# Seven of eight products in the last pass of a fused attention and two feed-forward layers

## The chip, the core and the metric

The kernel runs on one core of one Trainium2 chip. The metric is the device time of one execution in microseconds (us). The engines named here are PE (TensorE matmul), PEld (its weight load), DVE (VectorE), ACT (ScalarE), POOL (GpSimd) and SP (SyncE, which issues the DMAs). Inputs and output are float32.

## What is computed

A banded attention over 1536 tokens (2 batches of 768, 8 heads of 64) gives x of 1536 x 512. Two feed-forward layers of 512 to 2048 to 512 follow. In the reference, cut to what matters:

```python
x = attn_out.transpose(0, 2, 1, 3).reshape(B * S, H * D)      # 1536 x 512
h = np.maximum(x @ w_in, 0.0)                                 # first layer
x = h * h @ w_out
h = x @ w_in                                                  # second layer, beta = 1
g = np.where(h >= beta, h, np.where(h <= -beta, 0.0, (h + beta) ** 2 / (4.0 * beta)))
return g @ w_out
```

## The kernel before

**Three matmuls for one.** A float32 value is held as two fp32r parts, a high part and the rest (`Plan.copy` at L118 makes the high part, on ACT; `Plan.rest` at L130 subtracts it, on DVE). Each product is three matmuls into one sum in PSUM: high by high, low by high, high by low (`MOVING`).

**Chunks.** The 2048 inner columns are cut into 16 chunks of 128. The weights of a chunk (128 rows of `w_in` and of `w_out`, four blocks of 128 each) stand as high and low parts in one of nine slots (`slot0` to `slot8`, `h` and `l`). The program's names carry a further number that only counts tiles (`slot5l_128` is the low part of slot 5). From the second layer on slot 8 is cut up and used for the small g tiles, so eight slots are left.

**Events.** The work is a list of events (`Ffn.__init__`), each one chunk for one range of tokens. An event has a first product `h` (four blocks of 128 by three matmuls, L479), a function on ACT and DVE, and a second product `y` (L532), which adds to banks of PSUM that are kept over all 16 chunks. In the second layer the tokens are done in two passes of 768: tokens 768 to 1535 with the chunks from 15 down to 0, then tokens 0 to 767 with the chunks from 0 up to 15, the last pass. In a pass every chunk has two events: one for 512 tokens (its `h` in bank 0, its `y` in banks 2 to 5) and one for 256 tokens (its `h` in bank 1, its `y` in banks 6 and 7). The last two chunks are put in another order.

**The function of the second layer** (L499, L501, L503) is `max(h, min(r, 1) * r)` with `r = relu(h / 2 + 1 / 2)`: one instruction on ACT, then two on DVE. Two more make the parts of g (L118 on ACT, L130 on DVE). For the 256 tokens r lies in the tile `nat` and g in `slot8`; for the 512 tokens they are `r` and `g`.

**Weights in the last pass.** Chunks 0 to 7 are in the eight slots when the pass begins. Chunks 8 to 15 are read back from DRAM (`kept`, written when they were first made, at L416 to L442) and split again into parts, two halves of 512 each (`Ffn.parts`).

**What sets the order.** The kernel records each operation with a length, a due time and the keys of what it reads and writes. `Plan.emit` then lays out all engines by these lengths and due times and writes the instructions in the order of their planned starts, each engine in order. Which instruction waits for which is settled from that written order: an instruction that touches a tile waits for the ones written before it that touch the same tile in a way that matters. A PSUM bank is one tile.

Of the kernel before, what the change touches and what calls it, by code (L numbers as in the profile page):

```python
# [307 lines left out]
class Ffn:  # L308
# [12 lines left out]

    KF = 16
    CB = 4

    def __init__(self, nc, plan, banks, x, w, half, kept, out):
# [24 lines left out]
        for t0, order in ((768, down), (0, up)):  # L350
            parts = [(n, o) for n in range(self.KF) for o in (0, 512)]

            if not t0:
                parts[-4:] = [(n, o) for o in (512, 0) for n in (self.KF - 2, self.KF - 1)]
            for n, o in parts:
                hb = 1 if o or not t0 and n == self.KF - 1 else 0
                event(1, order[n], t0 + o, 256 if o else 512, hb, [6, 7] if o else y,
                      n == 0, n == self.KF - 1, 256 if o else 512)

        at = 0  # L360
        for e in self.events:
            e["due"] = at
            e["len"] = e["n"] / 512
            at += e["len"]
# [13 lines left out]
    def plan_slots(self, span):  # L378


        holds = [None] * len(self.slots)
        used = [-9] * len(self.slots)
        span = [(first - 9 * (first == 0), end) for first, end in span]
        self.makes = []
        keys = [(e["layer"], e["c"]) for e in self.events]
        for u, key in enumerate(keys):
            slots = [i for i, (first, end) in enumerate(span) if first <= u < end]
            found = [i for i in slots if holds[i] == key]
            if found:
                i = found[0]  # L390
            else:
                later = keys[u:]
                free = [i for i in slots if used[i] < u - 2]
                i = max(free, key=lambda i: (
                    later.index(holds[i]) if holds[i] in later else len(keys), -used[i], -i))
                self.makes.append((u, max(used[i], span[i][0] - 2)))
                holds[i] = key
            self.events[u]["slot"] = i
            used[i] = u


        self.due_makes = [keys[u] for u, _ in self.makes]

    def make_after(self, u):

        while self.makes and self.makes[0][1] <= u:
            self.make(self.makes.pop(0)[0])

    def make(self, u):

        nc, op = self.nc, self.plan.op
        e = self.events[u]
        layer, c, due = e["layer"], e["c"], e["due"]
        kc, f32 = self.ring("whole")
        if (layer, c) in self.stored:
            op("dma", 1456, due - W_LOAD, lambda: nc.sync.dma_start(out=f32, in_=self.kept[c]),  # L416
               [("kept", c)], [(*kc, 0), (*kc, 1)], lag=LAG)
            self.due_makes.pop(0)
            self.parts(u, kc, f32)
            return  # L420
# [22 lines left out]
        later = any(key == (layer, c) for key in self.due_makes[1:])  # L443
# [5 lines left out]
        self.parts(u, kc, f32)  # L449

    def parts(self, u, kc, f32):
        plan = self.plan
        e = self.events[u]
        i = e["slot"]
        sl = self.slots[i]
        for n in range(2):
            src, hi, lo = f32[:, 512 * n:512 * n + 512], sl[0][:, n], sl[1][:, n]
            d = e["due"] - W_MAKE + 0.4 * n
# [7 lines left out]
    def h(self, u):  # L466

        nc, op = self.nc, self.plan.op
        assert all(v != u for v, _ in self.makes)
        e = self.events[u]  # L470
        layer, t0, N, kb, i = e["layer"], e["t0"], e["n"], e["hb"], e["slot"]
# [25 lines left out]
        else:  # L497

            op("act", ns_act(N) + 64, due, lambda: nc.scalar.activation(  # L499
                out=r, in_=hp, func=ACTF.Relu, bias=self.half, scale=0.5), [bank], [kr])  # L500
            op("dve", ns_dve(N), due, lambda: nc.vector.scalar_tensor_tensor(  # L501
                out=r, in0=r, scalar=1.0, in1=r, op0=ALU.min, op1=ALU.mult), (), [kr], port=True)
            op("dve", ns_dve(N), due, lambda: nc.vector.tensor_tensor(  # L503
                out=r, in0=hp, in1=r, op=ALU.max), [bank], [kr])
        self.plan.copy(N, due, g[:, 0], r, [kr], [(*kg, 0)], engines=GCOPY)
        self.plan.rest(N, due, g[:, 1], r, g[:, 0], [kr, (*kg, 0)], [(*kg, 1)], engines=GREST)
        self.g[u] = kg, g

    def y(self, u):

        op, plan, nc = self.plan.op, self.plan, self.nc
        e = self.events[u]
        layer, t0, N, yb, i = e["layer"], e["t0"], e["n"], e["yb"], e["slot"]
# [4 lines left out]
        for t in range(self.CB if layer == 0 else N // P):  # L518
# [40 lines left out]
            else:  # L559
                ko, ot = self.ring("o")  # L560
                r0 = t0 + t * P
                for n in range(2):
                    h = slice(256 * n, 256 * n + 256)
                    way = ("act", "dve")[n]
                    plan.copy(256, due, ot[:, h], o[:, h], [bank], [(*ko, n)], psum=True, engines=(way,))
                op("dma", 728, due, lambda ot=ot, r0=r0: nc.sync.dma_start(
                    out=self.out[r0:r0 + P, :], in_=ot), [(*ko, n) for n in range(2)], (), lag=LAG)

    def run(self, events):

        for u in events:
            if u == 0:
                self.make_after(-1)
                self.h(0)
            if u + 1 < len(self.events):
                self.h(u + 1)
            self.y(u)
            self.make_after(u)

# [380 lines left out]
def kernel(  # L960
# [31 lines left out]
    def tiles(s, f, plan):  # L992
# [24 lines left out]
        f.tiles["o"] = [nat[:, 512 + i * 512:1024 + i * 512] for i in range(7)]  # L1017
        f.later = {
# [13 lines left out]
        }  # L1032
        if plan is None:
            return a
# [129 lines left out]
```

## Time and profile before

| | us |
|---|---|
| median of three runs | 639.33 |
| lowest and highest | 638.82 and 640.70 |
| the profiled execution | 640.03 |
| span in its profile | 638.2 |
| busy in it: PE, DVE, ACT | 625.1, 411.5, 308.3 |

The page of the profile gives busy times and shares; the chain of waits lists what ended last, in order of time; the stretches give busy time between two moments; the timeline lists single instructions with their start and length. Times in the trace count from the span's start. Matmuls overlap in the records, each being shown longer than the distance to the next one, so the pace of PE is read from start to start. The same holds of DVE and ACT where an instruction doesn't depend on the one before it.

### The profile page before, as it was taken

How to read it: one execution, taken by the hardware profiler on the slowest of the kernel's cores; microseconds unless marked ns; L12 is line 12 of the kernel's file. 1: busy time of each engine (PE TensorE's matmuls, PEld its weight loads, DVE VectorE, ACT ScalarE, POOL GpSimd, SP SyncE). 2: the span in 40 equal slices, each digit the busy share in tenths (PEclk: the TensorE clock that was granted, in tenths of full speed). 3: DMA queues.
4: the chain of work that ended last, by engine and by line, in shares of the span. 5: the costliest groups of instructions: out<-in, count | busy, mean ns of one | idle time of the engine just before them, and what ended most of it. 6: DMA issues, size and time to landing. Idle time of an engine off the chain costs nothing.

```text
span 638.2 us, 9469 instructions
## 1 busy us (share of the span) xinstructions
PE 625.1 (98%) x3535; PEld 512.6 (80%) x3535; DVE 411.5 (64%) x949; ACT 308.3 (48%) x668; POOL 30.1 (5%) x57
## 2 busy tenths in 40 slices
PE   7999999999999999999999999999999999999995
PEld 5788987878888888888888888888888888888883
DVE  5899999965459992242299999964443555543443
ACT  3898777855456642232256565533222443332232
POOL 3122020110000000000000000000000000000000
PEclk9999999999999999999999999999999999999998
DMA  7444454430123583000016624121000311100002
GB/s 266 155 156 153 133 150 148 145 139 17 34 99 101 181 251 129 0 1 0 1 33 207 221 67 163 35 67 34 0 1 1 106 61 66 34 1 0 2 1 105
DMA packets 18775, 55.23 MB, mean 87 GB/s; under 512 B 2336, under 2 KB 2336, under 8 KB 18720
## 3 DMA queue, kind: packets, MB, share of 16 engines
q1 hardware_dynamic: 18432, 54.53, 26.0%
q8 instruction: 30, 0.49, 0.3%
q14 instruction: 25, 0.20, 0.1%
q10 hardware_dynamic: 288, 0.00, 0.0%
HBM read 47.19 MB, written 7.34 MB: 85 GB/s over the span
## 4 chain that ended last, share of the span: by engine, by line
PE 94%; DVE 3%; DMA 1%; ACT 1%; issue 0%; ACTq 0%; DVEq 0%
PE bank L479 42%; PE bank L532 41%; PE bank L639 4%; PE bank L726 3%; PE bank L690 3%; DMA words<-in_n_global_dram 1%; DVE pr L662 0%; PE bank L1068 0%; DVE whole L435 0%; DVE whole L439 0%; PE bank L1066 0%; ACT g L118 0%; DVE m L144 0%; DVE whole L432 0%; DVE slot0l L130 0%
## 5 line engine op out<-in xcount | busy, mean ns | idle before, releaser
L501 DVE SCALAR_TENSOR_TENSOR r<-r 128x512 f32<-128x512 f32 x32 | 22.2, 692 | 88.8 <-ACT r L499 88.6
L118 ACT ACTIVATE g<-r 128x512 fp32r<-128x512 f32 (+1 forms) x84 | 51.4, 612 | 50.6 <-DVE r L503 29.1
L495 DVE SCALAR_TENSOR_TENSOR r<-bank,r 128x512 f32<-128x512 f32 (+1 forms) x52 | 33.8, 649 | 61.7 <-ACT r L494 59.7
L130 DVE TENSOR_TENSOR g<-r,g 128x512 fp32r<-128x512 f32 (+1 forms) x84 | 56.0, 667 | 24.2 <-ACT g L118 20.4
L499 ACT ACTIVATE r<-bank,half 128x512 f32<-128x512 f32 x32 | 22.0, 689 | 96.4 <-PE bank L479 96.4
L494 ACT ACTIVATE r<-bank 128x512 f32<-128x512 f32 (+1 forms) x52 | 29.3, 564 | 76.9 <-PE bank L479 75.6
L667 ACT ACTIVATE pr<-pr,mn 128x256 f32<-128x256 f32 (+1 forms) x96 | 45.8, 480 | 11.2 <-DVE mn L662 10.8
L142 ACT ACTIVATE whole<-raw 128x512 f32<-128x512 f32 x50 | 33.4, 675 | 13.6 <-DMA kept<-whole 2.2
L662 DVE CUSTOM_DVE_ANT_0 pr<-bank,m 128x256 f32<-128x256 f32 (+1 forms) x96 | 33.2, 394 | 5.1 <-PE bank L726 5.1
L479 PE MATMUL bank<-x,slot1h 128*128 128x512 f32 (+1 forms) x120 | 34.2, 351 | 0.0
L479 PE MATMUL bank<-x,slot0h 128*128 128x512 f32 (+1 forms) x120 | 34.0, 352 | 0.2 <-DVE x L130 0.2
L439 DVE SCALAR_TENSOR_TENSOR whole<-raw,whole 128x512 uint32<-128x512 uint32 x50 | 34.1, 684 | 0.1
L479 PE MATMUL bank<-x,slot3h 128*128 128x512 f32 (+1 forms) x120 | 34.1, 353 | 0.0
L435 DVE SCALAR_TENSOR_TENSOR whole<-raw,whole 128x512 uint32<-128x512 uint32 x50 | 33.9, 684 | 0.2
L479 PE MATMUL bank<-x,slot2h 128*128 128x512 f32 (+1 forms) x120 | 34.0, 352 | 0.0
L479 PE MATMUL bank<-x,slot4h 128*128 128x512 f32 (+1 forms) x112 | 33.5, 365 | 0.0
L479 PE MATMUL bank<-x,slot6h 128*128 128x512 f32 (+1 forms) x112 | 33.4, 365 | 0.0
L479 PE MATMUL bank<-x,slot5h 128*128 128x512 f32 (+1 forms) x112 | 33.3, 365 | 0.0
L639 PEld LDWEIGHTS bank<-nat 64*128 64x128 f32 x352 | 25.1, 206 | 8.8 <-issue 3.0
L639 PE MATMUL bank<-nat 64*128 64x128 f32 x352 | 29.8, 306 | 2.0 <-DMA nat<-in_q_dram 1.0
L146 POOL TENSOR_SCALAR pr<-pr,mn 128x256 f32<-128x256 f32 (+1 forms) x39 | 25.4, 660 | 130.1 <-DVE mn L674 55.6
L479 PE MATMUL bank<-x,slot7h 128*128 128x512 f32 (+1 forms) x88 | 25.5, 357 | 0.0
(264 smaller groups left out, 1564.4 us busy)
## 6 DMA issues: line engine op xcount, KB each, us to landing
raw<-in_moe_w_in_dram SPq DMA_DIRECT2D x25, 512.0 KB, 3.5
raw<-in_moe_w_out_dram SPq DMA_DIRECT2D x25, 512.0 KB, 4.5
pr<-in_moe_w_in_dram SPq DMA_DIRECT2D x7, 512.0 KB, 3.4
pr<-in_moe_w_out_dram SPq DMA_DIRECT2D x7, 512.0 KB, 4.0
nat<-in_k_dram SPq DMA_DIRECT2D x12, 256.0 KB, 3.8
nat<-in_q_dram SPq DMA_DIRECT2D x12, 256.0 KB, 3.2
nat<-in_v_dram SPq DMA_DIRECT2D x12, 256.0 KB, 3.4
out_dram<-nat SPq DMA_DIRECT2D x12, 256.0 KB, 2.5
```

The source lines that it names most:

```text
L118: ("act", ns_act(n) - 30 * psum, lambda: nc.scalar.activation(out=out, in_=in_, func=ACTF.Copy), False),
L130: ways = [("dve", ns_dve(n), lambda: nc.vector.tensor_tensor(out=out, in0=in_, in1=hi, op=ALU.subtract), not psum)]
L142: ("act", ns_act(n) + (0 if isinstance(by, float) else 107), lambda: nc.scalar.activation(out=out, in_=in_, func=ACTF.Copy, scale=by), False),
L435: op("dve", ns_dve(512), d + 0.2, lambda h=h: nc.vector.scalar_tensor_tensor(out=word[:, h], in0=low[:, h], scalar=29, in1=word[:, h], op0 ...
L439: op("dve", ns_dve(512), d + 0.3, lambda h=h: nc.vector.scalar_tensor_tensor(out=word[:, h], in0=high[:, h], scalar=0x80000000, in1=word[: ...
L479: op("pe", ns_mm(N), due + 0.01 * m, lambda k=k, a=a, b=b, m=m: nc.tensor.matmul(out=hp, lhsT=sl[a][:, 0, k * P:(k + 1) * P], rhs=self.x[: ...
L494: op("act", ns_act(N), due, lambda: nc.scalar.activation(out=r, in_=hp, func=ACTF.Relu), [bank], [kr])
L495: op("dve", ns_dve(N), due, lambda: nc.vector.scalar_tensor_tensor(out=r, in0=hp, scalar=0.0, in1=r, op0=ALU.max, op1=ALU.mult), [bank], [kr])
L532: lambda o=o, lhsT=lhsT, rhs=rhs, n=n: nc.tensor.matmul(out=o, lhsT=lhsT, rhs=rhs, start=(e["first"] and n == 0), stop=(e["last"] and n == 2),
L639: nc.tensor.matmul(**c)
L662: op("dve", ns_dve(w), due, lambda e=e: nc.vector.tensor_tensor_reduce(out=pr[:, e, :w], in0=self.banks[kbs[e % 2]][:, e // 2 * 256:e // 2 ...
L667: op("act", ns_act(w) + 200, due, lambda e=e: nc.scalar.activation(out=pr[:, e, :w], in_=pr[:, e, :w], func=ACTF.Exp, bias=mn[:, e:e + 1], ...
```

## The change

It concerns the last pass alone. Chunks 0 and 1 keep their events. Chunks 2 to 15 go in seven pairs. For a pair the first product of the 512 tokens is a product of 512 tokens by 512 inputs with 512 inputs by 256 columns. Each is cut in two by two parts: 256 tokens, 256 inputs (two blocks), 128 columns (one chunk). Strassen's algorithm in Winograd's form makes it from seven products instead of eight. They are called P1 to P7 in the code. Each has six matmuls of 256 tokens (two blocks by three) and goes into one of four areas, each a half of bank 0 or bank 1 (area 0 and 1 in bank 0, 2 and 3 in bank 1).

- **Sums of the inputs** (`combined`): four DVE instructions make the sums of parts of x in place in `save0`, where x of these tokens lies in float32. Four copies and four rests split them into x[768:1280], which the pass before no longer needs. This is done once.
- **Sums of the weights** (`make_sums`): for each pair the two `w_in` chunks are read again from `kept`, four subtractions of 256 make the sums, one copy and one rest of 1024 split them into a slot of their own. A pair so needs three slots, and its two chunks and its sums are loaded when the pair before the last user of the slot is through.
- **Sums of the products** (`add`): one copy on ACT and seven additions on DVE, each of 256 from a PSUM area, give the four parts of h. The function then works on four parts of 256, from SBUF instead of PSUM.
- **The 256 tokens** keep their plain product (`rest256`): twelve matmuls each for the first and second chunk of the pair, in areas 2 and 3 (here called h0 and h1), with functions z0 and z1.
- **The order** in a pair is given by due times in `STEPS`, in units of the length of a 512-token event: P1, P6, P5, then the second products `y` of the pair before with its first chunk, P2, P7, `y` with its second chunk, P4, P3, and h0 and h1 with the second products of the 256 tokens (banks 6 and 7) between.

```diff
+    PAIR = 2.885
+    STEPS = dict(P1=0, P6=0.12, P5=0.24, y0=0.38, P2=0.88, P7=1, y1=1.13, P4=1.63, P3=1.75, h0=1.89, z0=2.14, z1=2.39, h1=2.64)
+    LAST = dict(STEPS, h0=1.4, h1=2.3)
...
             if not t0:
-                parts[-4:] = [(n, o) for o in (512, 0) for n in (self.KF - 2, self.KF - 1)]
+                parts = parts[:4]
...
+        self.combine = len(self.events) - 4
+        for c in range(2, self.KF, 2):
+            self.events.append(dict(layer=1, c=c, pair=(c, c + 1), t0=0, n=768, last=c + 2 == self.KF))
...
+    def make_sums(self, key, i, due):
...
+        for n in range(2):
+            c = key[2] + n
+            assert (1, c) in self.stored
+            op("dma", 728, due - W_LOAD, lambda n=n, c=c: nc.sync.dma_start(
+                out=f32[:, 512 * n:512 * n + 512], in_=self.kept[c][:, 0:512]), [("kept", c)], [(*kc, n)], lag=LAG)
...
+        for n, (out, in0, in1) in enumerate(((t1, b12, b11), (t3, b22, b12), (t2, b22, t1), (t4, b21, t2))):
+            op("dve", ns_dve(256), due - W_MAKE + 0.1 * n, lambda out=out, in0=in0, in1=in1: nc.vector.tensor_tensor(
+                out=out, in0=in0, in1=in1, op=ALU.subtract), [(*kc, 0), (*kc, 1)], [kt], port=True)
...
+        plan.copy(1024, due - W_MAKE + 0.6, hi, t, [kt], his, engines=WCOPY)
+        plan.rest(1024, due - W_MAKE + 0.7, lo, t, hi, [kt] + his, los, engines=WREST)
...
+    def combined(self):
...
+        for n, (out, in0, in1, f) in enumerate((
+                (b2, b1, b2, ALU.add), (b1, a1, b1, ALU.subtract), (a1, b2, a1, ALU.subtract), (a2, a2, a1, ALU.subtract))):
+            op("dve", ns_dve(512), due - 6 + n, lambda out=out, in0=in0, in1=in1, f=f: nc.vector.tensor_tensor(
+                out=out, in0=in0, in1=in1, op=f), (), keys, port=True)
+        for k in (0, 1, 2, 3):
+            hi, lo = (self.x[:, b, k, 768:1280] for b in range(2))
...
+            plan.copy(512, due + 0.1 * k, hi, t[:, k], [keys[k]], xh, engines=ACOPY)
+            plan.rest(512, due + 0.1 * k, lo, t[:, k], hi, [keys[k]] + xh, xl, engines=AREST)
...
+    def pair_h(self, u):
...
+        regions = [(0, 0), (0, 256), (1, 0), (1, 256)]
+        area = [self.banks[kb][:, o:o + 256] for kb, o in regions]
...
+            def products():
+                for m, (lhsT, rhs) in enumerate(calls):
+                    nc.tensor.matmul(out=area[region], lhsT=lhsT, rhs=rhs, start=(m == 0), stop=(m == len(calls) - 1))
+
+            op("pe", len(calls) * ns_mm(256), start + due, products, reads, [("area", region)])
...
+        def add(out, key, region, in1, k1, due):
+            op("dve", ns_dve(256), start + due, lambda: nc.vector.tensor_tensor(
+                out=out, in0=area[region], in1=in1, op=ALU.add), [("area", region)] + [k for k in (k1,) if k != key], [key])
...
+        def rest256(n):
...
+            product(2 + n, whole(512, w, range(4)), step[f"h{n}"])
+            kr, r = self.ring("r256")
+            kg, g = self.ring("gz")
+            self.three(256, start + d[f"h{n}"], area[2 + n], [("area", 2 + n)], r, kr, True)
+            self.halves(256, start + d[f"h{n}"], r, kr, g, kg)
+            out["z", n] = kg, g
...
+        product(0, whole(0, "c", (0, 1)), step["P1"])
+        product(1, sums(0, (0, 1), 1), step["P6"])
+        product(2, sums(256, (2, 3), 0), step["P5"])
+        self.plan.copy(256, start + d["P1"], p, area[0], [("area", 0)], [kp], psum=True, engines=("act",))
+        add(u2, k2, 1, p, kp, d["P6"])
+        product(0, whole(0, "c", (2, 3)), step["P2"])
+        product(3, sums(256, (0, 1), 2), step["P7"])
+        add(p, kp, 0, p, kp, d["P2"])
+        function((0, 0), p, [kp], False, d["P2"])
+        add(u3, k3, 3, u2, k2, d["P7"])
+        add(u2, k2, 2, u2, k2, d["P7"])
+        product(1, sums(256, (2, 3), 3, is_sum=False), step["P4"])
+        product(3, [(0, k, True, "d", 0, k * P) for k in (2, 3)], step["P3"])
+        add(u4, k4, 1, u3, k3, d["P4"])
+        function((0, 1), u4, [k4], False, d["P4"])
+        add(u3, k3, 2, u3, k3, d["P7"] + 0.01)
+        function((1, 1), u3, [k3], False, d["P7"] + 0.01)
+        add(u2, k2, 3, u2, k2, d["P3"])
+        function((1, 0), u2, [k2], False, d["P3"])
+        for n in range(2):
+            rest256(n)
...
+    def pair_y(self, u):
...
+            kb = (2, 3, 4, 5, 6, 7)[t]
...
+        if last:
+            for t in (4, 5, 0, 1, 2, 3):
+                for n in range(2):
+                    product(n, t, 0.1 + (t % 4 + 2 * (t < 4)) * 0.25 + 0.1 * n)
+            return
+        for n in range(2):
+            for t in range(4):
+                product(n, t, step[f"y{n}"] + 0.04 * t)
+            for t in (4, 5):
+                product(n, t, step[f"z{n}"] + 0.04 * t - 0.16)
```


The places that follow are from the programs as built, in each engine's own order.

**PE, from one chunk to the next.** Before, in the last pass, the 256-token product of one chunk (bank 1, slot 2) ends, the 512-token product of the next (bank 0, slot 1) begins, and the second product of the first (banks 2 to 5) follows:

```order
L479 MATMUL bank1_64<-x_73,slot2l_122 128x256
L479 MATMUL bank1_64<-x_73,slot2h_121 128x256
L479 MATMUL bank0_63<-x_73,slot1h_119 128x512
L479 MATMUL bank0_63<-x_73,slot1l_120 128x512
L532 MATMUL bank2_65<-slot2h_121,g0_110 128x512
L532 MATMUL bank3_66<-slot2h_121,g0_110 128x512
```

Now, at the head of the third pair (chunks 6 and 7, their weight sums in slot 6), right behind h1 of the second pair (bank 1) and P1 (bank 0, slot 0), stand the end of P6 in bank 0, then P5 in bank 1, then `y` of the second pair, whose g lies in free columns of x:

```order
L602 MATMUL bank0_63<-x_73,slot6l_130 128x256
L602 MATMUL bank0_63<-x_73,slot6h_129 128x256
L602 MATMUL bank1_64<-x_73,slot6h_129 128x256
L602 MATMUL bank1_64<-x_73,slot6l_130 128x256
L602 MATMUL bank1_64<-x_73,slot6h_129 128x256 x2
L602 MATMUL bank1_64<-x_73,slot6l_130 128x256
L602 MATMUL bank1_64<-x_73,slot6h_129 128x256
L673 MATMUL bank2_65<-slot2h_121,x_73 128x512 x2
```

Between the last matmul of h1 and the first of P5, both in bank 1, twelve matmuls of 256 now stand.

**DVE at the same moment.** Before, around the end of a chunk, DVE has the function and g of the 512 tokens and then of the 256 tokens (`nat`, `slot8`) and of the next chunk:

```order
L130 TENSOR_TENSOR g1_111<-r1_113,g1_111 128x512
L501 SCALAR_TENSOR_TENSOR nat_115<-nat_115 128x256
L503 TENSOR_TENSOR nat_115<-bank1_64,nat_115 128x256
L130 TENSOR_TENSOR slot8l_134<-nat_115,slot8l_134 128x256
L501 SCALAR_TENSOR_TENSOR r0_112<-r0_112 128x512
```

Now, at the head of the third pair, the first row is the last step of z0 of the second pair (bank 1), then come a rest of g, the rest of 1024 of the weight sums of chunks 8 and 9, a rest of z0, and the two steps of z1, the second of which reads bank 1:

```order
L550 TENSOR_TENSOR nat_115<-bank1_64,nat_115 128x256
L130 TENSOR_TENSOR x_73<-r1_113,x_73 128x256
L130 TENSOR_TENSOR slot5l_128<-raw1_107,slot5h_127 128x1024
L130 TENSOR_TENSOR slot8h_133<-nat_115,slot8h_133 128x256
L548 SCALAR_TENSOR_TENSOR nat_115<-nat_115 128x256
L550 TENSOR_TENSOR nat_115<-bank1_64,nat_115 128x256
```

In the built program the first of these rows waits for the last matmul of h1, and P5 on PE waits for the last of them.

**PE in the middle of a pair.** Before, six matmuls of `y` (banks 6 and 7) stand between the end of a product in bank 0 and the next one in bank 1, which was read long before:

```order
L479 MATMUL bank0_63<-x_73,slot2h_121 128x512
L532 MATMUL bank6_69<-slot3h_123,slot8l_134 128x512 x2
L532 MATMUL bank6_69<-slot3l_124,slot8l_134 128x512
L532 MATMUL bank7_70<-slot3h_123,slot8l_134 128x512 x2
L532 MATMUL bank7_70<-slot3l_124,slot8l_134 128x512
L479 MATMUL bank1_64<-x_73,slot2h_121 128x256
```

Now, in the third pair, three matmuls stand between P3 (bank 1, slot 7) and h0 (bank 1 too, slot 0):

```order
L602 MATMUL bank1_64<-x_73,slot7h_131 128x256 x2
L602 MATMUL bank1_64<-x_73,slot7l_132 128x256
L602 MATMUL bank1_64<-x_73,slot7h_131 128x256
L673 MATMUL bank6_69<-slot2h_121,slot8h_133 128x512 x2
L673 MATMUL bank6_69<-slot2l_122,slot8h_133 128x512
L602 MATMUL bank1_64<-x_73,slot0h_117 128x256
```

In the built program h0 waits for the second of two DVE additions from bank 1, of which the first waits for the last matmul of P3.

## Rows read from the trace of the kernel before

**Rows 1.** The page: busy us (share of the span) and instructions; TensorE's granted clock in tenths

```profile
PE 625.1 (98%) x3535; PEld 512.6 (80%) x3535; DVE 411.5 (64%) x949; ACT 308.3 (48%) x668; POOL 30.1 (5%) x57
PEclk9999999999999999999999999999999999999998
```

**Rows 2.** The chain of waits by time, last pass: start, length, engine, tile, line, matmuls

```profile
566.14 1.88 PE bank L479 x14
568.01 2.77 PE bank L532 x12
570.78 2.33 PE bank L479 x10
574.50 1.87 PE bank L479 x14
```

**Rows 3.** Stretches of the last pass: length, busy us of the engines, PE clock, DMA

```profile
560.00:575.00 15.00, 15.00 (x75) 12.40 (x74) 6.60 (x14) 4.20 (x8) 0.00 (x0) 1.00 0.00 1
575.00:590.00 15.00, 15.00 (x76) 12.37 (x75) 5.49 (x11) 3.79 (x8) 0.00 (x0) 1.00 0.00 0
590.00:605.00 15.00, 15.00 (x79) 12.46 (x78) 6.52 (x12) 4.31 (x8) 0.00 (x0) 1.00 0.01 2
```

**Rows 4.** Groups by line and shape, 500 to 640: count, busy us, mean ns, idle before

```profile
L130 DVE TENSOR_TENSOR g<-r,g 128x512 fp32r<-128x512 f32 x16 | 11.1, 692 | 5.4 <-ACT g L118 4.6
L499 ACT ACTIVATE nat<-bank,half 128x256 f32<-128x256 f32 x16 | 7.6, 476 | 4.1 <-PE bank L479 4.1
L503 DVE TENSOR_TENSOR nat<-bank,nat 128x256 f32<-128x256 f32 x16 | 6.8, 425 | 0.5
L501 DVE SCALAR_TENSOR_TENSOR nat<-nat 128x256 f32<-128x256 f32 x16 | 6.7, 419 | 4.2 <-ACT nat L499 4.2
L130 DVE TENSOR_TENSOR slot8h<-nat,slot8h 128x256 fp32r<-128x256 f32 x8 | 3.4, 423 | 2.1 <-ACT slot8h L118 1.9
L118 ACT ACTIVATE slot8h<-nat 128x256 fp32r<-128x256 f32 x8 | 3.3, 418 | 6.3 <-DVE nat L503 6.3
```

**Rows 5.** Timeline of PE, ACT, DVE after a 256-token product: start, length, instruction

```profile
565.97 0.28 PE L479 MATMUL bank<-x,slot6h 128*128 128x256 f32 x1
...
567.26 0.28 PE L479 MATMUL bank<-x,slot6h 128*128 128x256 f32 x1
...
567.38 0.40 PE L479 MATMUL bank<-x,slot5h 128*128 128x512 f32 x1
...
567.63 0.47 ACT L499 ACTIVATE nat<-bank,half 128x256 f32<-128x256 f32 x1
...
568.30 0.42 DVE L501 SCALAR_TENSOR_TENSOR nat<-nat 128x256 f32<-128x256 f32 x1
...
568.75 0.42 DVE L503 TENSOR_TENSOR nat<-bank,nat 128x256 f32<-128x256 f32 x1
...
569.21 0.42 ACT L118 ACTIVATE slot8h<-nat 128x256 fp32r<-128x256 f32 x1 [1.10 <-DVE nat L503]
```

**Rows 6.** Timeline of DVE where instructions don't depend on each other

```profile
402.57 0.42 DVE L130 TENSOR_TENSOR slot8h<-nat,slot8h 128x256 fp32r<-128x256 f32 x1
402.91 0.68 DVE L439 SCALAR_TENSOR_TENSOR m<-pr,m 128x512 uint32<-128x512 uint32 x1
403.51 0.42 DVE L432 TENSOR_SCALAR m<-m 128x512 uint32<-128x512 uint32 x1
```

**Rows 7.** Timeline of the last chunk: PE waiting for g, then the four tiles leaving

```profile
626.85 0.63 ACT L118 ACTIVATE g<-r 128x512 fp32r<-128x512 f32 x1 [1.49 <-DVE r L503]
627.01 0.39 PE L532 MATMUL bank<-slot0l,g 128*128 128x512 f32 x1
...
627.53 1.42 PE L532 MATMUL bank<-slot7h,g 128*128 128x512 f32 x5
...
629.23 1.75 ACT L118 ACTIVATE nat<-bank 128x256 f32<-128x256 f32 x4 [1.75 <-PE bank L532]
```

**Rows 8.** DMA issues: tiles, queue, count, size each, median us to landing

```profile
whole<-kept SPq DMA_DIRECT2D x5, 512.0 KB, 3.4
```

More of the change, by code (lines that the diff above doesn't have):

```diff
@@ L384, in plan_slots @@
         self.makes = []
[L385 to L399, printed above, removed]
@@ L402, in plan_slots @@
-        self.due_makes = [keys[u] for u, _ in self.makes]
+        keys = [
+            [(1, c) for c in e["pair"]] + [(1, "sums", e["c"])] if "pair" in e else [(e["layer"], e["c"])]
+            for e in self.events]
+        for u, need in enumerate(keys):
+            later = sum(keys[u:], [])
+            got = []
+            for key in need:
+                slots = [i for i, (first, end) in enumerate(span) if first <= u < end]
+                found = [i for i in slots if holds[i] == key]
+                if found:
+                    i = found[0]
+                else:
+                    free = [i for i in slots if used[i] < u - 2 + (len(need) > 1)]
+                    i = max(free, key=lambda i: (
+                        later.index(holds[i]) if holds[i] in later else len(later), -used[i], -i))
+                    self.makes.append((u, max(used[i], span[i][0] - 2), key, i))
+                    holds[i] = key
+                got.append(i)
+                used[i] = u - (key[1] == "sums")
+            self.events[u]["slot"], self.events[u]["slots"] = got[0], got
@@ L442, in make @@
             ), [(*kr, n)], [(*kc, n)], port=True)
[L443 removed]
+        later = any(k == key or layer and k[1] == "sums" and c - k[2] in (0, 1) for k in self.due_makes[1:])
         self.due_makes.pop(0)
@@ L497, in h @@
         else:
[L499 to L504, printed above, removed]
+            self.three(N, due, hp, [bank], r, kr, True)
@@ new lines, in pair_y, with product @@
+    def pair_y(self, u):
+        op, nc = self.plan.op, self.nc
+        e = self.events[u]
+        out = self.g.pop(u)
+        last, step = e["last"], self.STEPS
+        def product(n, t, due):
+            kg, g = out["z", n] if t > 3 else out[n, t // 2]
+            kb = (2, 3, 4, 5, 6, 7)[t]
+            o, i, cs = self.banks[kb], e["slots"][n], slice(t % 2 * P, t % 2 * P + P)
+            for m, (a, b) in enumerate(MOVING):
+                op("pe", ns_mm(512), e["due"] + due + 0.01 * m, lambda a=a, b=b, m=m: nc.tensor.matmul(
+                    out=o, lhsT=g[:, a, cs], rhs=self.slots[i][b][:, 1], start=False, stop=(last and n == 1 and m == 2),
+                ), [(("hi", "lo")[b], i, 1), (*kg, a)], [("bank", kb)])
+            if last and n:
+                self.leave(o, ("bank", kb), t * P, e["due"] + due + 0.05)
+        if last:
[8 more added lines that the diff above has]
+                product(n, t, step[f"z{n}"] + 0.04 * t - 0.16)
@@ L559, in y, with leave @@
             else:
[L560 to L567, printed above, removed]
+                self.leave(o, bank, t0 + t * P, due)
+    def leave(self, o, bank, r0, due):
+        plan, nc = self.plan, self.nc
+        ko, ot = self.ring("o")
+        for n in range(2):
+            h = slice(256 * n, 256 * n + 256)
+            way = ("act", "dve")[n]
+            plan.copy(256, due, ot[:, h], o[:, h], [bank], [(*ko, n)], psum=True, engines=(way,))
+        plan.op("dma", 728, due, lambda: nc.sync.dma_start(
+            out=self.out[r0:r0 + P, :], in_=ot), [(*ko, n) for n in range(2)], (), lag=LAG)
     def run(self, events):
```

113 lines of the change are left out of this document (99 added, 14 removed).

## The prediction

> **What bounds the kernel now.** I read the page first: PE is busy 98% of the span at its full granted clock in nearly every slice [rows 1]. The chain of waits by time shows what the last pass is made of: fourteen first-product matmuls in 1.88 us (twelve of 256 tokens and two of 512), twelve second-product ones in 2.77, ten first-product ones of 512 in 2.33, and six more second-product ones before the same pattern begins again at 574.50, 8.36 us after 566.14 [rows 2]. No idle piece stands between. The stretches say the same from the other side: PE is busy 15.00 us of 15.00, DVE 5.5 to 6.6, ACT about 4, and the DMA engines hardly at all [rows 3]. So a column less on PE is time saved, as long as DVE and ACT, which have more than half of their time free, stay off the path. The question is whether they do.
>
> **PE's own work.** The pace of a first-product matmul is 2.33 / 10 = 0.233 us for 512 tokens [rows 2] and (567.38 - 565.97) / 12 = 0.1175 us for 256 [rows 5]. For a pair of chunks 24 matmuls of 512 (5.59 us) become 7 x 6 = 42 of 256 (4.94 us). That is 0.66 us less in a pair, **4.6 us less** in seven. The other 60 matmuls of a pair (24 of 256 tokens, 36 of the second product) stay. A pair goes from 16.73 us (two of 8.36) to 16.07 us of PE work.
>
> **Work that has cover.** The sums of x are four DVE additions and four rests of 512, 8 x 0.69 = 5.5 us once [rows 4], laid beside chunks 0 and 1, where DVE has 8 or 9 of 15 us free [rows 3]: nothing. If that cover were gone it would be 5.5 us. The weight sums are read again from DRAM, 14 DMAs of 256 KB; a read of twice the size lands in 3.4 us [rows 8], the DMA engines are idle [rows 3], and they are issued about a pair (16 us) ahead: nothing. Without that lead it would be up to 3.4 us for each pair.
>
> On DVE a pair has 7 additions, 12 function and rest steps of the four parts, 6 of z0 and z1 and 4 subtractions, which are 29 of 256, a rest of 1024, and four rests of 512 where the chunks are not in a slot. Instructions that don't depend on each other start 0.34 us apart at 256, and 0.60 at 512 (402.57 to 402.91 to 403.51) [rows 6]. No row has 1024 elements. The line through 423 ns at 256 and 692 ns at 512 [rows 4] gives 1.23 us; one instruction of 512 (0.69) and two of them (1.38) are the ends. I take 1.23, with the next start 1.15 later. In all 29 x 0.34 + 1.15 + 4 x 0.60 = 13.4 us of 16.07. ACT has 13 of 256 at 0.42 to 0.48, one of 1024 and four of 512, some 9.5 us. Neither is the bound by its sum. It is single waits that count.
>
> **The waits, step by step.** The steps come from the rows. From the start of a product's last matmul to the start of the instruction that reads the bank it is 0.37 us (567.26 to 567.63). A DVE step that depends on the one before starts 0.45 later (568.30 to 568.75), and ACT goes on 0.04 after DVE's end (569.17 to 569.21) [rows 5]. PE goes on 0.05 after the end of what it waited for (626.85 + 0.63 = 627.48 to 627.53) [rows 7]. The four areas are halves of two banks, and in the built program every wait is by whole bank, as front shows for P5 and h0; in the first pair P6 even waits for ACT's copy out of the other half of its bank.
>
> 1. *h0 behind P3.* h0 goes into area 2, which the second of two additions on DVE reads last, and the first of them waits for P3. From the start of P3's last matmul: 0.37 + 0.34 + 0.42 + 0.05 = 1.18 us until h0 may start. PE has 0.12 and three matmuls of 0.231 (2.77 / 12), 0.81. It stands for 0.37 us, in pairs two to seven: **2.2 us**.
>
> 2. *P5 at the head of a pair.* The last step of z0 was written behind h1, so it waits for h1's last matmul although it reads the other half. From that matmul's start: last step of z0 at 0.37, rest of g 0.71, rest of 1024 at 1.05, rest of z0 2.20, first step of z1 2.54, its second 2.99, end 3.41, PE 3.46. PE comes to P5 after 0.12 + 12 x 0.1175 = 1.53. So the third pair stands for 1.9 us. In the fourth and sixth the rest of g isn't between, 1.6 each. In the fifth P5 is written ahead of z1's second step: 0. The seventh has no weight sums there, and z1 itself decides: 0.37 + 0.48 on ACT + 0.04 + 0.45 + 0.42 + 0.05 = 1.8, so 0.3. Together **5.4 us**.
>
> 3. *The first two pairs*, where less stands between. First pair: P4 directly follows P2 in bank 0 and waits for an addition behind P2, 0.37 + 0.42 + 0.05 = 0.84, against 0.12 + 0.23 on PE: 0.5. P3 waits for an addition ten DVE places behind the one that P4 lets go, 0.37 + 8 x 0.34 + 2 x 0.45 + 0.42 + 0.05 = 4.46, against 0.12 + 12 x 0.1175 + 9 x 0.231 = 3.6: 0.9. h1 waits for ACT's step on h0, behind one addition and one other step on ACT, 0.37 + 0.42 + 0.04 + 0.4 + 0.48 + 0.05 = 1.75, against 0.12 + 6 x 0.231 = 1.5: 0.25. That is **1.7**. Second pair: P6 needs the low part of its weight sums. That rest of 1024 is the eighth DVE instruction behind the step that waits for h1, at about 3.4, so it is done at 4.7; PE is there after 0.12 + 0.7 + 11 x 0.231 + 0.12 = 3.5: 1.2. P2, behind an addition that stands behind another rest of 1024, 0.3: **1.5**.
>
> 4. *The end.* The chain of z0 and z1 of the last pair has less cover than the last chunk had: I put 0.7 us, where the kernel before stands for 0.3 (627.01 + 0.23 to 627.53) [rows 7]: **+0.4**. Four tiles left together before, 1.75 us of copies [rows 7]; now one is left to the last: **-0.5**.
>
> The sum is -4.6 + 2.2 + 5.4 + 1.7 + 1.5 + 0.4 - 0.5 = **+6.1 us**. On the profiled execution (640.03) that is 646.1; on the median of the runs (639.33) **645.4**. Ends: with the rest of 1024 at 0.69 the four waits behind it shrink by 0.54 each, 643.2. With PE losing a whole matmul's pace (0.12) at each of some 19 waits, since the weights can't be loaded ahead there, 647.7; with the longer rest as well, 648.3.
>
> **A rule of the Trainium skill.** In the kernel before, first products alternate between bank 0 and bank 1, with matmuls of other banks between, and no row shows a wait of PE there [rows 2]. The Trainium skill (PSUM — Partial Sum Buffer, "PSUM bank collisions raise a hardware error") asks to guard PSUM by bank and quadrant, not by address. By it two halves of one bank are no two buffers, which speaks against four areas in two banks, and the waits of the built program obey it. Waits by address would give the second rival's time.
>
> **Rivals.** *Everything is covered:* all waits end before PE comes to them. Time 639.33 - 4.6 - 0.5 = **634.2**, faster. For it: DVE's 13.4 of 16.07 us and PE without idle time today. Against: z1's own chain, 1.8 us, is longer than the 1.53 that PE needs to P5; it decides for this rival only if P5 were nowhere behind z1. I give 0.05.
>
> *Waits by halves:* if z0's last step did not wait for h1 and P5 only for area 2, point 2 would go, and about 1 us of point 3: 645.4 - 5.4 - 1 = **639.0**, no change. The waits of the built program speak against it: 0.08.
>
> *DVE becomes the bound:* if the steps are so interleaved that each takes its full length, a pair with weights needs 29 x 0.42 + 1.23 + 4 x 0.69 = 16.2 us, and DVE's own waits for h1 and P3, some 2.5 us, come on top: 18.7 against 16.07. Four such pairs cost 10.5 us in place of points 1 and 2 there (1.5 + 5.1), so 645.4 + 3.9 = **649.3**. For it: many steps of a chain of 256 depend on the one before. Against: two chains are interleaved in the order. 0.12.
>
> **How the numbers follow.** The forecast, slower by some 6 us, has 0.75; 643.2 to 648.3 are its ends. The range 641.5 to 649.0 takes it in and half of the third rival. 0.3% (1.9 us) is about what a measurement of this kernel can tell from no change. Faster by more: 0.06. Within: 0.09. Slower by more: 0.85, which is the forecast and the third rival.
>
> **What would show it.** Right: PE's share in the last pass falls, with idle time of 1.6 to 1.9 us before the first products in bank 1 at the head of three pairs, named as waiting for DVE's L550, 0.4 us before h0 six times behind L607, and 0.1175 us as the pace of the new matmuls. Wrong: if PE shows no idle time at P5, the waits were not as I read them; if the pace of the six-matmul groups is above 0.12 us, the first term is too big; if DVE has no idle time in the last pass, the third rival holds; if P5's wait is there but shorter by half a microsecond, the rest of 1024 was mis-sized.

## The result, and the profile after

The changed kernel takes 647.89 us (median of four runs, 647.28 to 649.12). Beside it, the kernel before took 639.50 (638.82 to 640.70). The ratio is 1.0132, with a 95% interval of 1.011 to 1.0153. The forecast was 645.4, so the direction held and the size was 2.5 us short. The profiled execution has a span of 646.2 us against 638.2.

The page, its busy times and the granted clock, answers to [rows 1]:

```profile
PE 622.5 (96%) x3661; PEld 514.8 (80%) x3661; DVE 453.9 (70%) x1083; ACT 322.9 (50%) x714; POOL 29.9 (5%) x57
PEclk8999999999999999999999999999999999999998
```

PE is busy 2.6 us less, and the span is 8 us longer. Stretches of the last pass answer to [rows 3] (length, busy us of PE, PEld, DVE, ACT and POOL, clock, DMA):

```profile
550.00:565.00 15.00, 13.48 (x84) 11.69 (x83) 12.79 (x31) 7.77 (x17) 0.00 (x0) 1.00 0.11 35
565.00:580.00 15.00, 13.78 (x90) 12.16 (x90) 11.87 (x29) 7.93 (x16) 0.00 (x0) 1.00 0.32 109
```

PE, which was busy for 15.00 of 15, now idles for up to 1.5 us of a stretch, and DVE's share has almost doubled. What PE waited for in the whole pass is in the table of its waits (total us, times, longest). The kernel before has no row in the same table.

```profile
PE bank L602 <- DVE nat L550: 4.5, 3, 1.7
PE bank L602 <- DVE raw L607: 2.5, 5, 1.2
PE bank L602 <- DVE slot5l L130: 1.0, 1, 1.0
PE bank L673 <- ACT slot8l L118: 0.3, 1, 0.3
```

The chain of waits shows the largest one, P5 at the head of the third pair (start, length, what). Where [rows 2] had PE pieces end to end, there is now this between two of them:

```profile
541.17 0.42 DVE nat L550
541.60 0.34 DVE x L130
541.93 1.13 DVE slot5l L130
543.07 0.34 DVE slot8h L130
543.40 0.35 DVE nat L548
...
543.77 0.44 DVE nat L550
544.21 0.04 issue
544.25 0.98 PE bank L602 x6
```

This is step for step the chain of the prediction's point 2: z0's last step, a rest of g, the rest of 1024, a rest of z0, the two steps of z1, then P5.

**The account.** I set the start of a chunk against the end of the pass. From the first product of chunk 1 to the last matmul the kernel before needs 630.17 - 503.69 = 126.48 us, the changed one 638.93 - 504.17 = 134.76: 8.28 more. The pass begins 0.48 later, and after the last matmul 7.27 us are left instead of 8.03. That makes +8.0. The four matmuls, before and then after, in the timeline of PE:

```profile
503.69 0.63 PE L479 MATMUL bank<-x,slot5h 128*128 128x512 f32 x2
...
630.17 0.39 PE L532 MATMUL bank<-slot7l,g 128*128 128x512 f32 x1
```

```profile
504.17 0.63 PE L519 MATMUL bank<-x,slot5h 128*128 128x512 f32 x2
...
638.93 0.39 PE L673 MATMUL bank<-slot4l,g 128*128 128x512 f32 x1
```

The waits below are distances from start to start beyond the pace of the matmul before (0.1175 or 0.232 us).

| term | forecast | measured |
|---|---|---|
| PE's own work | -4.6 | -4.5 (shown by a run without waits, below) |
| h0 behind P3, pairs 2 to 7 | +2.2 | 5 x 0.31 + 1.38 = +2.9 |
| P5, pairs 3 to 7 | +5.4 | 1.87 + 1.54 + 0 + 1.54 + 0.30 = +5.3 |
| first pair (P4, P3, h1) | +1.7 | 0.45 + 0.86 + 0.18 = +1.5 |
| second pair (P6, P2) | +1.5 | 1.15 + 0.18 = +1.3 |
| wait at the end | +0.4 | 0.48 - 0.29 = +0.2 |
| first weight load after a wait | in the ends only | 15 x 0.10 = +1.5 |
| ahead of the last pass | 0 | +1.2 (the change) - 0.7 (this execution's start) = +0.5 |
| after the last matmul | -0.5 | -0.8 |
| sum | +6.1 | +7.9 of 8.0 |

Two terms are new. A matmul that has waited is followed by the next one 0.22 us later instead of 0.1175. The timeline (start, length, engine) shows what differs: in the run of the work a weight load starts 0.11 us ahead of its matmul, and behind the wait both start together.

```profile
541.45 0.19 PEld L602 LDWEIGHTS bank<-x,slot0h 128*128 128x128 f32 x1
...
541.56 0.28 PE L602 MATMUL bank<-x,slot0h 128*128 128x256 f32 x1
...
544.25 0.19 PEld L602 LDWEIGHTS bank<-x,slot6h 128*128 128x128 f32 x1 [1.92 <-DVE nat L550]
544.25 0.39 PE L602 MATMUL bank<-x,slot6h 128*128 128x256 f32 x1 [1.72 <-DVE nat L550]
...
544.48 0.28 PE L602 MATMUL bank<-x,slot6l 128*128 128x256 f32 x1
```

The other is the half microsecond before the pass. It is one execution set against one, and the experiment with six more writes takes it apart.

### The profile page after: what moved, and what is told of

Read it like the earlier page. It is cut to its first block, busy times and chain, and to the rows that moved or that the text cites. A ratio compares the mean times of both kernels' runs of the same rounds, so it can differ in the third digit from the quotient of the medians.

```text
span 646.2 us, 9946 instructions
## 1 busy us (share of the span) xinstructions
PE 622.5 (96%) x3661; PEld 514.8 (80%) x3661; DVE 453.9 (70%) x1083; ACT 322.9 (50%) x714; POOL 29.9 (5%) x57
## 4 chain that ended last, share of the span: by engine, by line
PE 81%; DVE 10%; DMA 4%; ACT 3%; issue 1%; SPq 0%; ACTq 0%; DVEq 0%
PE bank L519 29%; PE bank L715 29%; PE bank L602 7%; PE bank L673 7%; PE bank L829 3%; PE bank L916 3%; PE bank L880 2%; DMA kept<-whole 2%; DVE raw L607 1%; DMA whole<-kept 1%; DVE nat L550 1%; DMA words<-in_n_global_dram 1%; DVE whole L475 1%; DVE whole L479 1%; DVE pr L852 1%
## 5 line engine op out<-in xcount | busy, mean ns | idle before, releaser
L548 DVE SCALAR_TENSOR_TENSOR r<-r 128x256 f32<-128x256 f32 (+1 forms) x46 | 24.0, 528 | 34.0 <-ACT r L546 33.9
L142 ACT ACTIVATE whole<-raw 128x512 f32<-128x512 f32 x50 | 33.2, 672 | 21.0 <-DMA kept<-whole 8.1
L546 ACT ACTIVATE r<-bank,half 128x512 f32<-128x512 f32 x18 | 12.4, 686 | 45.7 <-PE bank L519 45.7
L607 DVE TENSOR_TENSOR raw<-bank,raw 128x256 f32<-128x256 f32 x49 | 20.0, 421 | 18.9 <-PE bank L602 17.7
L546 ACT ACTIVATE r<-raw,half 128x256 f32<-128x256 f32 x28 | 13.3, 505 | 32.7 <-DVE raw L607 32.5
L519 PE MATMUL bank<-x,slot6h 128*128 128x512 f32 (+1 forms) x96 | 29.3, 370 | 0.0
L519 PE MATMUL bank<-x,slot5h 128*128 128x512 f32 (+1 forms) x96 | 29.2, 370 | 0.0
L519 PE MATMUL bank<-x,slot3h 128*128 128x512 f32 (+1 forms) x88 | 25.8, 360 | 0.6 <-DVE r L550 0.6
L519 PE MATMUL bank<-x,slot1h 128*128 128x512 f32 (+1 forms) x88 | 25.7, 357 | 0.2 <-ACT slot1h L118 0.2
L519 PE MATMUL bank<-x,slot0h 128*128 128x512 f32 (+1 forms) x88 | 25.5, 358 | 0.2 <-DVE x L130 0.2
L519 PE MATMUL bank<-x,slot2h 128*128 128x512 f32 (+1 forms) x88 | 25.6, 358 | 0.0
```

Source lines behind the costliest of these rows:

```text
L519: op("pe", ns_mm(N), due + 0.01 * m, lambda k=k, a=a, b=b, m=m: nc.tensor.matmul(out=hp, lhsT=sl[a][:, 0, k * P:(k + 1) * P], rhs=self.x[: ...
```

## The experiments

My theory was that the waits come from the order of the instructions against banks that have not yet been read, and that each has its own local cause. The rival was that DVE has too much to do in a pair, so that a wait which is removed turns up at the next place. Line numbers differ by a few between these kernels.

### P5 behind y0

```diff
-    STEPS = dict(P1=0, P6=0.12, P5=0.24, y0=0.38, ...
+    STEPS = dict(P1=0, P6=0.12, P5=0.74, y0=0.24, ...
```

> Two due times are exchanged: P5 now follows the second products y0 instead of standing before them. Theory (the place in the order): PE then has 1.4 + 2.8 us between h1's last matmul and P5, more than the 2.9 to 3.5 us that z1's second step on DVE needs, so the waits of 1.9, 1.5, 1.5 and 0.35 us at P5 go, and with three of them 0.1 us each for the weight load: 647.9 - 5.6 = 642.3 us. Rival (DVE itself is too slow in a pair): the wait turns up at the next product that needs DVE, P2 or P4, and the time stays within 1 us of 647.9.

647.79 us (646.59 to 649.33), ratio 1.0129 (1.0106 to 1.0153). My theory missed, and the rival's number came, though the wait did not turn up at P2 or P4. In the table of PE's waits, P5's row (DVE L550) is gone, and that of L607 has grown from 2.5 to 6.2 us:

```profile
PE bank L602 <- DVE raw L607: 6.2, 6, 3.0
```

All of the growth is at h0 in the third and fourth pair, 2.14 and 3.11 us (0.31 and 1.38 in the changed kernel). The chain of waits before h0 of the third pair names a read of weights, which could be issued only when the subtractions of the sums before had left the buffer:

```profile
547.43 0.42 DVE raw L443
...
548.30 4.35 DMA whole<-kept
...
552.74 0.42 DVE raw L443
...
553.61 0.77 DVE raw L607 x2
...
554.41 2.63 PE bank L602 x12
```

P5's wait had been cover for this read. And h0's twelve matmuls took 2.63 us there, where they took 1.67 behind the short wait of the changed kernel. Stretches around the two waits (columns as above; the clock is the last number but two) show the granted clock fall behind them:

```profile
551.00:554.40 3.40, 1.44 (x10) 0.95 (x8) 2.48 (x6) 1.71 (x3) 0.00 (x0) 1.00 0.14 53
554.40:557.00 2.60, 2.58 (x13) 2.59 (x14) 2.33 (x7) 1.45 (x4) 0.00 (x0) 0.58 0.00 0
...
571.80:575.20 3.40, 0.45 (x3) 0.02 (x2) 2.20 (x6) 1.98 (x4) 0.00 (x0) 1.00 0.03 11
575.20:577.90 2.70, 2.70 (x13) 2.70 (x14) 2.62 (x8) 1.30 (x4) 0.00 (x0) 0.52 0.00 0
```

The matmuls behind each of the two waits, h0's and the next three or so, lose 1.5 us in this way against their pace elsewhere. The median of this kernel is a mixture: two of its four executions took 646.59 and 646.66 us at a mean granted clock of 0.995, the other two, of which the profiled one is the first, 648.91 and 649.33 us at 0.989 and 0.987. So part of what ate up the gain is the clock, and not in every execution.

### Keys by bank

```diff
-  op("pe", ..., products, reads, [("area", region)])
+  op("pe", ..., products, reads, [("bank", region // 2)])
```

The readers (`add`, the copy of P1, the function of h0 and h1) get the same key. No instruction is added or removed.

> The planner is told of banks instead of areas: the keys of the first products and of their readers are the bank, nothing else. Theory (the order was written without knowing these waits): it puts other matmuls ahead of a product whose bank isn't read out yet, so P5 stands behind seven or eight matmuls of y0 and h0 behind two to four of 512 in most pairs. The four waits at P5 (5.3 us) go, most of h0's (2.9 us) and some 0.5 to 1 us of the first two pairs' 3.1: 639 to 641 us. Rival (DVE itself is too slow): 647 to 648 us, the waits only stand elsewhere.

636.10 us (635.71 to 636.47), ratio 0.995 (0.9933 to 0.9966): 11.8 us less than the changed kernel, and faster than the kernel before. PE has no row left in the table of waits of the last pass. A stretch of it:

```profile
535.00:550.00 15.00, 15.00 (x93) 13.08 (x91) 13.73 (x34) 7.41 (x16) 0.00 (x0) 1.00 0.34 107
```

DVE runs the same 1083 instructions in 453.5 us, with three load buffers as before. So the rival falls: DVE has room for this work, and what cost the time is the order on all engines together. From the third pair on, P5 now stands behind five to eight matmuls of `y0`, and in the pairs three to six h0 stands behind five to seven of 512, where three stood. The first experiment had moved only P5, against `y0`.

### The rest of 1024 cut, in two ways

```diff
-  plan.rest(1024, ..., lo, t, hi, ...)
+  plan.rest(128, ..., lo[:, 0:128], t[:, 0:128], hi[:, 0:128], ...)
```

> The rest of 1024 of the weight sums is cut to its first 128 columns (the low parts of the sums are then stale, part of the work is left out), the order otherwise as it was. It measures what this one DVE instruction costs where it stands between h1 and the last step of z1. Theory: it is 0.9 us of the waits at P5 in the third, fourth and sixth pair and of P6's in the second, so these fall from 1.9, 1.5, 1.5 and 1.2 to 0.9, 0.6, 0.6 and 0.2: 647.9 - 3.7 = 644.2 us. Rival (z1's own chain of steps sets P5's start, whatever else DVE does): P5's waits stay at 1.5 us and only P6's falls, 647 us.

649.56 us, ratio 1.0162 (1.0145 to 1.0179): slower, and it tells nothing about the rest, since the shorter length in the plan moved the order elsewhere. In the third pair two rests of 512 (slots 3 and 4, 0.60 each) now stood between h1 and z1, and P5 waited 1.61 us. So I ran it again with the plan's length kept at 1024 and the instruction cut to 256 columns:

> The rest of 1024 of the weight sums works on its first 256 columns only (the other low parts are stale, part of the work is left out), in the order that the changed kernel has, which the run without the rest had changed. Theory A (this instruction stands between h1 and the last step of z1 and so lengthens P5's wait): the waits at P5 in the third, fourth and sixth pair fall by 0.8 us each, P6's in the second by 0.8 and P2's by 0.2: 647.9 - 3.4 = 644.5 us. Theory B (in the third and fourth pair a read of weights lands late and PE waits for it at h0 anyway): there the gain comes back at h0, and 1.8 us are left: 646.1 us. Rival (z1's own steps set P5's start): only P6 and P2 gain, 646.9 us.

644.79 us (643.97 to 646.41), ratio 1.0094 (1.008 to 1.0109): theory A. P5 waits 1.07, 1.01 and 1.01 us where it waited 1.87, 1.54 and 1.54, P6's wait is gone, and h0's in the fourth pair falls a little as well (1.11). Of the 0.8 us expected at P5 the third pair gave 0.8, the fourth and sixth 0.5: there the DVE rest of z0 starts only 0.57 us after the short rest, not 0.34, since it now waits for ACT's copy of z0. The table of PE's waits:

```profile
PE bank L603 <- DVE nat L551: 2.6, 3, 0.9
PE bank L603 <- DVE raw L608: 2.4, 6, 0.9
```

### Six more writes in the kernel before, and half of them

```diff
-  later = any(key == (layer, c) for key in self.due_makes[1:])
+  later = any(key == (layer, c) for key in self.due_makes[1:]) or layer and 1 < c < 8
```

> The kernel before, with one thing of the change alone: chunks 2 to 7 of the second layer are written to DRAM too (six writes of 512 KB), though nothing reads them. Theory: ACT waits for these writes before it may fill the buffers again, weights come late, and PE loses 0.5 us between 380 and 400 us: 640.0 us, and the last pass starts 0.5 us later than the 503.85 of the kernel before. Rival (the half microsecond before the last pass comes from the sums of x): 639.5 us, start at 503.85.

640.37 us (ten runs), ratio 1.002 (1.0011 to 1.003). The writes cost about 1 us of median. In the profile PE loses most of it from 380 to 400 us. The same stretch of four kernels, in this order: before, before with the writes, changed, and keys by bank with half writes (the next experiment):

```profile
380.00:400.00 20.00, 20.00 (x105) 16.91 (x104) 19.64 (x38) 11.06 (x20) 0.00 (x0) 1.00 0.55 181
```

```profile
380.00:400.00 20.00, 19.33 (x101) 15.95 (x101) 18.38 (x35) 10.89 (x20) 0.00 (x0) 1.00 0.75 235
```

```profile
380.00:400.00 20.00, 19.41 (x98) 15.93 (x97) 18.46 (x36) 10.93 (x19) 0.00 (x0) 1.00 0.74 238
```

```profile
380.00:400.00 20.00, 20.00 (x106) 16.69 (x104) 19.40 (x37) 11.28 (x20) 0.00 (x0) 1.00 0.70 216
```

ACT may not fill a buffer again before its write has landed (L142 waits for `kept<-whole` 4.7 us there, against 1.4), DVE's conversion follows late, and PE waits 0.7 us for a function step behind it. Even so the last pass began no later in that profile than in the kernel before, at 503.40 us against 503.69 (not 503.85, as the expectation has it), against the expectation's second mark. An earlier matmul, the first of a second product near 318 us, shows what made up for it. It stands in the same place of the same order in the kernel before, the one with the writes (with the start of its pass) and the changed one, in this order:

```profile
317.96 0.40 PE L532 MATMUL bank<-g,slot8h 128*128 128x512 f32 x1
```

```profile
316.79 0.40 PE L532 MATMUL bank<-g,slot8h 128*128 128x512 f32 x1
...
503.40 0.63 PE L479 MATMUL bank<-x,slot5h 128*128 128x512 f32 x2
```

```profile
317.24 0.40 PE L715 MATMUL bank<-g,slot8h 128*128 128x512 f32 x1
```

The execution with the writes was 1.2 us ahead there, and the changed one 0.7, a lead that both have by 32 us, from the same instructions on PE. From this matmul to the pass they then need 0.9 and 1.2 us more than the kernel before (185.73 us). So the writes' cost is about a microsecond in the profiles too, and the +0.5 of the account is +1.2 for the change and -0.7 for an early start that belongs to the execution. The sums read only 512 of 1024 columns, so half of each write can go:

```diff
+  cols = 1024 if full else 512
...
-  nc.sync.dma_start(out=self.kept[c], in_=f32)
+  nc.sync.dma_start(out=self.kept[c][:, 0:cols], in_=f32[:, 0:cols])
```

> The planner's keys are banks, as before, and chunks 2 to 7 are written with the 512 columns that the sums read, instead of 1024: six writes of 256 KB. Theory (the writes of these chunks hold up the loads of the pass before): 0.3 to 0.8 us less than the 636.1 of bank keys alone, 635.5 us. Rival: the writes cost nothing, 636.1 us.

634.75 us (633.79 to 635.81), ratio 0.9928 (0.9916 to 0.994). The loss at 380 to 400 is gone, as the last of the four rows shows, with the sums of x still made: so the six writes cost it, and not these sums. The interval overlaps that of bank keys alone by a little.

### The loads

P5 behind y0 as in the first experiment, and the sums' reads left out:

```diff
-  lambda n=n, c=c: nc.sync.dma_start(out=f32[...], in_=self.kept[c][:, 0:512])
+  lambda: None
```

> P5 behind y0 again, and the fourteen reads of weights for the sums are left out (the subtractions then work on what lies in the buffer, part of the work is left out), in the same order. Theory (a read can be issued only when its buffer is free, lands 4 to 6 us later, and the subtraction that waits for it stands ahead of the additions for h0 on DVE): the waits of 2.1 and 3.1 us at h0 go back to 0.3, and with them the stretches of granted clock 0.5 to 0.6 behind them (1.5 us): 647.8 - 1.8 - 2.8 - 1.5 = 641.7 us. Rival (DVE has too much to do in these pairs): the waits at h0 stay, 647 us.

645.35 us, ratio 1.0104 (1.0089 to 1.0119): between the two. h0 still waits 1.55 and 2.55 us. The chain of waits now names the chunk's own read, which I had left in, for the same buffers:

```profile
563.61 5.62 DMA whole<-kept
...
569.31 0.64 ACT slot5h L118
...
570.67 0.34 DVE raw L442
```

So I gave all loads more buffers, which leaves nothing out:

```diff
+  spare = f.tiles["raw"][2].bitcast(F32).rearrange("p n t -> p (n t)")
+  for i in range(2):
+      f.tiles["whole"].append(spare[:, i * 1024:(i + 1) * 1024])
```

> P5 behind y0, and the loads of the last pass have five buffers instead of three (the third raw buffer, unused in this pass, gives two more); nothing is left out. Theory (all loads of a pair, the sums' reads and the chunks' own, are issued late because their buffer comes free late, and that takes the place of P5's wait): the waits of 2.1 and 3.1 us at h0 in the third and fourth pair go to 0.3, the stretches at half clock behind them go too, 641 to 642.3 us. Rival (DVE's own queue holds h0 back, the loads only look late): the waits at h0 stay above 1.5 us, 645 to 648 us.

643.79 us, ratio 1.0071 (1.0056 to 1.0087). h0 waits 0.93 and 1.54 us, and the clock stays at 1.00 behind it. Neither number came: the loads were more than half of it. The chain of waits before h0 of the third pair still has a read in it, now of 2.6 us, and behind it DVE's queue:

```profile
546.27 2.61 DMA whole<-kept
...
551.57 0.35 DVE raw L443
...
552.80 0.77 DVE raw L607 x2
```

How the remainder divides between the read and the queue, on which subtractions stand ahead of the additions for h0, stays open. In the changed kernel, with P5 where it was:

> The changed kernel with five buffers for the loads in place of three, P5 where it was. Theory (the loads cost only the 1.1 us at h0 of the fourth pair as long as P5's waits stand ahead of them): 646.8 us, P5's waits unchanged at 1.9, 1.5 and 1.5. Rival (late loads also lengthen P5's waits): these fall as well, below 645 us.

646.97 us (646.21 to 647.20), ratio 1.012 (1.0105 to 1.0136): the theory's number, though the interval overlaps that of the changed kernel, so the trace has to decide. P5's waits are unchanged (its row in the table is 4.5, 3, 1.7 again), and h0 in the fourth pair waits 0.31 instead of 1.38. So in the changed kernel the loads cost about 1 us, and once P5's wait is taken away they cost more: 4 us lie between 647.79 and 643.79. Of these 2.8 are the shorter waits at h0 in the two profiles; the rest goes with the clock, which stayed at 1.00.

### The order spread by bank

```diff
-  STEPS = dict(P1=0, P6=0.12, P5=0.24, y0=0.38, P2=0.88, P7=1, y1=1.13, P4=1.63, P3=1.75, h0=1.89, z0=2.14, z1=2.39, h1=2.64)
+  STEPS = dict(P1=0, P6=0.12, y0=0.24, P5=0.74, P2=0.88, P7=1, y1=1.13, P4=1.63, z0=1.75, P3=2, h1=2.14, z1=2.39, h0=2.64)
...
-  product(2 + n, whole(512, w, range(4)), step[f"h{n}"])
+  product(2 - n, whole(512, w, range(4)), step[f"h{n}"])
```

> As the run with half writes, and the order is spread by bank: h1 goes into bank 0 instead of 1, P5 is due behind y0, z0 between P4 and P3, z1 between h1 and h0, and the last second products begin with tiles 2 and 3. At least 1.4 us of matmuls then stand between a product and the next one in its bank wherever a chain of steps reads it. Theory (what is left of waits comes from neighbours in one bank): the ten pauses of 0.1 to 0.2 us go, 634.5 to 635.2 us, near the 634.2 of the case in which all is covered. Rival (these pauses are no cost of the order, or the reads of weights set in): no change or up to 1 us more than with half writes alone.

634.33 us (633.96 to 635.55), ratio 0.9926 (0.9913 to 0.9939). Two waits are left, 0.44 and 0.75 us. With five buffers:

> The best order so far (keys by bank, half writes, h1 in bank 0) with five buffers for the loads. Two waits of PE are left in that order, 0.4 and 0.75 us before P1 of the fourth and fifth pair, named as waiting for z1's last step. Theory (they come from late loads on DVE's queue, like those at h0): they go, 633.3 us. Rival (z1's own steps are too slow for 2.8 us of cover): they stay, 634.3 us.

634.18 us (633.78 to 635.28), ratio 0.9923 (0.9909 to 0.9937). PE's table of waits is empty, as the theory had it, but the gain in the median is too small to tell from none. Of the three fastest orders (634.75, 634.33, 634.18) none can be told from the others. The pass shows what the products are worth when nothing waits. The first product of chunk 1 and the last matmul, by the timeline of PE:

```profile
502.99 0.63 PE L521 MATMUL bank<-x,slot5h 128*128 128x512 f32 x2
...
624.58 0.39 PE L675 MATMUL bank<-slot4l,slot8l 128*128 128x512 f32 x1
```

121.59 us against 126.48 before: 4.89 less, of which 0.29 is the wait that the kernel before had at its end and 0.10 the weight load behind it. The rest is 4.5.

## Why the prediction was right, and where it was short

**PE's own work** (-4.6) was right; the run without waits gives 4.5.

**P5** (5.4 against 5.3) was right with its cause: the short rest took 0.8, 0.5 and 0.5 us off the three waits. The length of the full rest is in the groups of DVE by shape, 1.22 us where I had 1.23 from a line through two sizes of [rows 4]:

```profile
L130 DVE TENSOR_TENSOR slot6l<-raw,slot6h 128x1024 fp32r<-128x1024 f32 x4 | 4.9, 1218 | 0.1
```

**h0** (2.2 against 2.9): the step of 0.37 was 0.31, but the fourth pair has 1.38. The step that failed is the one under "work that has cover": I let the re-reads of weights cost nothing because they are issued "about a pair ahead" and [rows 8] shows 3.4 us to landing. They are not issued a pair ahead there. The buffer comes free only inside the same pair, and the landing took 5.8 us, as the chain of waits of the changed kernel shows ahead of that h0:

```profile
565.17 0.44 DVE raw L443
565.63 0.32 SPq L437
...
566.00 5.82 DMA whole<-kept
...
571.92 0.42 DVE raw L443
```

With five buffers this wait fell to the 0.31 of the other pairs. The bound that I named for it, up to 3.4 us a pair, is what the first experiment then came near (3.1).

**The first two pairs** (3.2 against 2.8) came as worked out, a few tenths smaller. So did the wait at **the end** (0.2 for 0.4), and what follows the last matmul gave back 0.8 for 0.5.

**The weight load behind a wait** was only one of the ends (0.12 at each of 19 waits). The 0.10 us at 15 waits belongs in the sum, and with it the forecast would have been 646.9.

**Ahead of the last pass** I had nothing. The change makes chunks 2 to 7 be written to DRAM, by the condition for `later`, a line that isn't among those shown; I counted the reads and not these writes. They cost 1.2 us in this profile, 0.9 in that of the kernel before with the writes, and 1.0 in its median.

**What was luck.** With the weight loads and a microsecond for the writes the forecast would have been 647.9, the number that was measured. That the rest fits to a tenth is luck: h0 was 0.7 too small, and the first two pairs and the end were 0.9 too big. The range held because its upper end counted a weight load at each wait (647.7); nothing in it stood for the writes.

**The rivals.** That everything is covered (634.2) was false for this order, and right for the same products in another, with half writes and five buffers: 634.2 was measured. Its runs go from 633.8 to 635.3, so the agreement to a tenth is chance. Waits by halves: the P5 row names z1's step, which reads the other half of the bank, so the built program waits by bank. The Trainium skill (PSUM — Partial Sum Buffer, "PSUM bank collisions raise a hardware error") asks to guard PSUM by bank and quadrant, not by address, and the wait of 1.87 us for the other half of the bank is such a guard. What the chip would do without it was not tried. DVE as the bound: refuted by the keys by bank.

## What to carry to other kernels

Where a planner orders the work, its keys must be as coarse as the waits that the program is built with; here that alone was worth 11.8 us and turned a loss into a gain. A wait that is removed alone may have been the cover of a transfer or a queue behind it, so read what is late next, buffers included, before counting on it. A changed condition for what is kept is a change in traffic, even far ahead of the code it serves.

## What the runs showed of the hardware

- Behind a wait, PE's next matmul came 0.22 us after the one that had waited instead of 0.1175, in the changed kernel each time. The weight load of the waiting matmul started with it there, and 0.11 us ahead of it in the run of the work.
- The granted clock fell to a mean of 0.58 and 0.52, towards the lower of its two levels (1.2 GHz), in the 2.6 and 2.7 us behind waits of 2.0 and 3.0 us. In the run without the sums' reads it stayed at 1.00 behind a wait of 2.4 us. Each fall cost about another microsecond at h0 (2.63 us for twelve matmuls instead of 1.67), and half of one behind it.
- A read from DRAM of 512 KB landed in 3.4 us in the kernel before [rows 8]; in the run without the sums' reads one took 5.6 us with another of its size issued 0.6 us before it, and in the changed kernel one of half its size took 5.8 us with three others in flight.
